# Decode attention over a streamed cache: the fourth K block in halves, finer waits at the first blocks, one more block in TensorE's loop, and Wo in five pieces

## The chip, the cores and the metric

One core of one Trainium2 chip. The metric is the device time of one execution in microseconds; a kernel's time is the median of its runs. The kernel before took 2521.9 us (median of three runs, 2521.62 to 2524.93).

## The reference, cut to what matters

One query token attends over a cache of 65,536 keys in each of 16 heads of size 256; a small gated MLP multiplies the result.

```python
xn = _layernorm(x)
q  = (xn @ wq).reshape(1, 1, 16, 256)              # x: 1 x 448
p  = softmax(einsum(q, k_cache) * 256 ** -0.5)     # k_cache, v_cache: 16 x 65536 x 256, bf16
s  = einsum(p, v_cache).reshape(1, 1, 4096) @ wo
g  = silu(silu(xn @ w1) @ w2)
out = x + s * g
```

The two caches are 1074 MB of the 1084 MB that come in. Every byte is used once.

## The kernel before

The caches are cut into 64 K blocks and 64 V blocks of 8.39 MB (128 partitions x 128 keys x 256 x bf16). Three buffers R[0..2] hold one block each. K block i goes into R[i % 3]; when its scores are done, **V block i is loaded over it**; when TensorE has summed V, K block i+3 is loaded over that. All loads are issued by SyncE on one queue, in the order K3 V2 K4 V3 K5 V4 ...

In the code `take` waits for a semaphore and takes off what it waited for; KB is 128 keys, HK 64 and SUB 32. The cuts leave lines out where `...` stands.

VectorE and ScalarE share the scores of a K block in four quarters of 32 keys: VectorE multiplies 13 keys in one wide product, which ScalarE then sums one by one, and does the other 19 (`ND`) itself. TensorE does the softmax's maximum, the query's broadcast and the 64 matmuls of a V block.

```python
def load_k(i, s):
    take(sp, vf[s])                      # TensorE has finished the V block in R[s]
    sp.dma_start(out=R[s][:, :], in_=block(Kd, i)).then_inc(kl[s], 16)
    sp.sem_inc(kh[s], 16)

def load_v(i, s):
    take(sp, kf[s])                      # VectorE has finished the K block in R[s]
    sp.dma_start(out=R[s][:, :], in_=block(Vd, i)).then_inc(vl[s], 16)

def dve_block(s, between=None):
    ...
    take(dve, kl[s], 16)
    for k in range(NSTEP):               # 4 quarters
        if k == NSTEP // 2:
            take(dve, kh[s], 16)
        ...                              # wide product for ScalarE, then ND products with sum
    # at the end: copy of S, .then_inc(kf[s], 1); maximum, .then_inc(rm, 1)

def pe_v(s):
    take(pe, pv)
    take(pe, vl[s], 16)
    pe_keys(psO, s, s, 0, KB, True, True, od)
    pe_mark().then_inc(vf[s], 1)
... # loads at the start, after w1 and wq
    load_keys(R[0], block(Kd, 0), 0, HK, kl[0])
    ...                                  # w2
    load_keys(R[0], block(Kd, 0), HK, KB, kh[0])
    load_k(1, 1)
    ...                                  # once w2 is used
    load_k(2, 2); load_v(0, 0); load_v(1, 1)
    # loop: load_k(i + s, s); load_v(i + s - 1, (s - 1) % NR)
... # the end: Wo in pieces of heads (0-5, 5-10, 10-14, 14-16) around the last parts of V63
    pe.wait_ge(wl[2], 16)
    project(h0, h0 + 2)                  # heads 10, 11
    t = pe_turn(tok=True)                # turns V63's sums
    ...
    project(h0 + 2, h1)                  # 12, 13
    pe.wait_ge(wl[3], 16)
    project(pieces[3][0], H1)            # 14, then 15 when its column is there
```

## Time and profile before

| | kernel before |
|---|---|
| time, median | 2521.9 us |
| span of the profiled run (its time was 2523.0) | 2521.1 us |
| bytes read | 1084.3 MB |
| share of the main DMA queue's packets in 16 engines' span | 99.6% |
| VectorE, ScalarE, TensorE busy | 89%, 57%, 46% |

The prediction below shows the lines and reads them: the DMA never rests but at the two ends and in two holes near 97 and 117 us. In the profile's lines PE is TensorE, PEld its weight loads, DVE VectorE, ACT ScalarE and SPq SyncE's queue. A window's line gives its length, then for PE, PEld, DVE, ACT and POOL (GpSimd) the busy time and the number of instructions, then TensorE's granted clock, the DMA's busy share and its GB/s.

One thing more is needed to follow the rest. A block's semaphore gets one increment from each of the sixteen DMA engines, and the trace records them singly: V0's sixteen came from 96.71 to 100.75 us in the kernel before. A packet of 65,536 bytes takes 2.42 us on its engine (the median of 15,872 in the trace of before), from the start to the end of the run, save the first ones after a pause (below). I call the time from the first to the last increment of a block the *spread*, and *the last engine* the one whose increment comes last. In these traces an engine that had fallen behind stayed behind: in the kernel before the spread was 1.5 us at every block from 199 to 335 us. It shrank where the others stood still, from 3.05 to 1.74 us from V1 to K3, at the hole. The consumer waits for the last engine (TensorE began with V0 at 100.64 us of the profile's time, 0.13 after its last increment), and the last landing of Wo stands in the chain that ends the run. Times of increments, here and in the prediction, count from a zero 0.24 us ahead of that of the profile's views; where the two are set against each other below, I have allowed for that; the prediction sets them against each other as they stand.

### The profile page before, as it was taken

The page shows a single profiled execution, that of the slowest core. Times are in us where ns is not written, and L with a number is a line of the kernel's source. Part 1 is how long each engine was busy: PE and PEld are TensorE (multiplying, and loading weights), DVE is VectorE, ACT ScalarE, POOL GpSimd, SP SyncE. Part 2 cuts the span into 40 slices and gives each one's busy share as a digit, 9 for nine tenths or more (in the row PEclk, how much of TensorE's full clock was granted, in tenths as well). Part 3 has the DMA queues.
Part 4 walks back from the last instruction along what each step waited for, and adds up shares of the span by engine and source line. Part 5 has one row for each costly group of instructions (what it writes and reads, how often), then busy time and mean ns, then how long its engine had stood idle before and what let it go on. Part 6 is the DMA issues. An engine that isn't in the chain of part 4 may idle for free. (4 is left out here: it accounts for less than half of the span.)

```text
span 2521.1 us, 29267 instructions
## 1 busy us (share of the span) xinstructions
PE 1151.9 (46%) x4738; PEld 438.2 (17%) x4738; DVE 2233.4 (89%) x10277; ACT 1445.9 (57%) x6996; POOL 1.9 (0%) x14
## 2 busy tenths in 40 slices
PE   3243544534535435345354353453543534534457
PEld 1111211111112112111121121121211211111122
DVE  6979889889898898898988988989989889889897
ACT  4656556556565565565655655655556556556564
POOL 0000000000000000000000000000000000000000
PEclk7666767767667677677676676766766767767678
DMA  9999999999999999999999999999999999999998
GB/s 424 402 433 433 433 433 433 434 432 433 435 434 436 435 436 434 434 433 434 435 433 433 433 433 433 433 433 433 433 436 435 436 436 434 434 433 435 433 423 353
DMA packets 22872, 1084.50 MB, mean 430 GB/s; under 512 B 2371, under 2 KB 4549, under 8 KB 4933
## 3 DMA queue, kind: packets, MB, share of 16 engines
q1 hardware_dynamic: 22850, 1084.30, 99.6%
q8 instruction: 5, 0.08, 0.0%
q14 instruction: 15, 0.11, 0.0%
q10 hardware_dynamic: 2, 0.00, 0.0%
HBM read 1084.29 MB, written 0.00 MB: 430 GB/s over the span
## 5 line engine op out<-in xcount | busy, mean ns | idle before, releaser
L276 ACT ACTIVATE R<-R 128x256 bf16<-128x256 bf16 x3328 | 1330.7, 401 | 754.4 <-ACTq L159 754.3
L254 DVE CUSTOM_DVE_ANT_0 R<-R,qcur 128x256 bf16<-128x256 bf16 x4864 | 1700.2, 417 | 0.0
L323 PE MATMUL bank<-R,PV 128*2 128x512 bf16 x4096 | 1032.1, 419 | 20.9 <-PEq L159 7.6
L243 DVE TENSOR_TENSOR R<-R,qcur 128x3328 bf16<-128x3328 bf16 x256 | 482.6, 1885 | 190.0 <-DVEq L159 189.9
L276 ACT ACTIVATION_READ_ACCUMULATOR R<-R 128x1 f32 x3328 | 619.9, 186 | 0.0
L335 PE MATMUL bank<-ident,rmax 128*1 128x128 bf16 x65 | 17.1, 263 | 1078.9 <-PEq L159 1078.9
L323 PEld LDWEIGHTS bank<-R,PV 128*2 128x2 bf16 x4096 | 367.3, 90 | 657.7 <-issue 218.4
L254 DVE DVE_READ_ACCUMULATOR2_ANT S<- 128x1 f32 x4864 | 384.1, 79 | 0.0
L335 PEld LDWEIGHTS bank<-ident,rmax 128*1 128x1 bf16 x65 | 5.2, 79 | 1083.4 <-issue 1083.3
L352 PE MATMUL bank<-eye,O 2*128 2x2 f32 x264 | 40.0, 252 | 231.3 <-PEq L159 231.3
L289 ACT ACTIVATE hist<-bank 128x1 f32 (+1 forms) x65 | 11.1, 171 | 204.4 <-ACTq L159 204.4
L352 PEld LDWEIGHTS bank<-eye,O 2*128 2x128 f32 x264 | 36.2, 207 | 248.6 <-issue 248.6
L219 DVE TENSOR_REDUCE gmax<-bank 1x1 bf16<-1x128 f32 x65 | 18.3, 281 | 38.1 <-DVEq L159 38.1
L236 DVE CAST qcur<-bank 128x256 bf16<-128x256 f32 x64 | 27.2, 425 | 24.6 <-DVEq L159 24.5
L310 ACT COPY hist<-bank 128x2 f32 (+1 forms) x66 | 10.5, 160 | 59.8 <-ACTq L159 59.8
L302 ACT COPY O<-bank 2x512 f32<-2x512 f32 x67 | 37.5, 559 | 12.4 <-ACTq L159 12.4
L291 ACT ACTIVATE PV<-S,hist 128x128 bf16<-128x128 f32 (+1 forms) x65 | 26.0, 399 | 13.4 <-ACTq L159 13.2
L366 PE MATMUL bank<-q,ident 8*128 (+1 forms) x63 | 24.3, 386 | 7.6 <-issue 1.7
L229 DVE COPY S<-S 128x128 f32<-128x128 f32 (+1 forms) x65 | 14.7, 226 | 9.5
L230 DVE TENSOR_REDUCE rmax<-S 128x1 bf16<-128x128 f32 (+1 forms) x65 | 18.2, 279 | 0.0
L341 PE MATMUL bank<-gmax,ones_row 1*128 1x1 bf16 x65 | 10.3, 158 | 4.6 <-PEq L159 0.9
L291 ACT ACTIVATION_READ_ACCUMULATOR PV<-S,hist (+1 forms) x65 | 12.1, 186 | 0.0
(68 smaller groups left out, 90.6 us busy)
## 6 DMA issues: line engine op xcount, KB each, us to landing
R<-in_A_k_cache_dram SPq DMA_DIRECT2D x4, 4096.0 KB, 24.2
R<-in_A_v_cache_dram SPq DMA_DIRECT2D x6, 2048.0 KB, 21.5
R<-in_A_wq_dram SPq DMA_DIRECT2D x1, 3072.0 KB, 12.7
R<-in_A_v_cache_dram SPq DMA_DIRECT2D x3, 1024.0 KB, 15.2
R<-in_A_wo_dram SPq DMA_DIRECT2D x2, 1120.0 KB, 18.4
R<-in_B_w_dram SPq DMA_DIRECT2D x1, 1568.0 KB, 27.1
R<-in_B_w_dram SPq DMA_DIRECT2D x1, 1344.0 KB, 5.8
R<-in_A_v_cache_dram SPq DMA_DIRECT2D x2, 512.0 KB, 16.4
```

The costliest lines, as they stand in the source:

```text
L219: dve.reduce_max(out=gmax[0:1, :], in_=ps_m[0:1, :], axis=AX.X).then_inc(gm, 1)
L230: dve.reduce_max(out=rmax[:, :], in_=S[:, c0:c1], axis=AX.X).then_inc(rm, 1)
L236: dve.tensor_copy(out=qcur[:, :], in_=ps_q).then_inc(sd, 1)
L243: m = dve.tensor_tensor(out=pair, in0=pair, in1=qcur[:, None, :].to_broadcast([P, NA, Dh]), op=ALU.mult,)
L254: ins = dve.tensor_tensor_reduce(out=Kv[:, c, :], in0=Kv[:, c, :], in1=qcur[:, :], scale=1.0, scalar=0.0, op0=ALU.mult, op1=ALU.add, accum ...
L276: ins = act.activation(out=prod, in_=prod, func=ACT.Identity, accum_out=S[:, c : c + 1],)
L291: act.activation(out=PV[s][:, c0:c1], in_=S2[:, c0:c1], func=ACT.Exp, bias=col(0, 1), scale=scale, accum_out=col(1, 2),).then_inc(pv, 1)
L302: act.copy(out=O[:, :], in_=po).then_inc(oc, 1)
L323: ins = pe.matmul(po, lhsT=PV[t][:, c : c + 2], rhs=R[s][:, c * Dh : (c + 2) * Dh], start=(start and c == k0), stop=(stop and c == k1 - 2),)
L335: pe.matmul(ps_m[0:1, :], lhsT=rmax[:, 0:1], rhs=ident[:, :], start=True, stop=True).then_inc(tm, 1)
L352: ins = pe.matmul(ps_t2[:, 2 * a : 2 * a + 2], lhsT=Ov[:, j, a, :], rhs=eye2[:, j, :], start=(j == 0), stop=(j == 1), is_transpose=True,)
L366: pe.matmul(ps_q, lhsT=ident[0:HP, at(j)].to_broadcast([HP, P]), rhs=q8[:, o : o + Dh] if isinstance(o, int) else q8[:, bass.ds(o, Dh)], s ...
```

## The change

Its intent: close the holes at the start by letting loads go out sooner, and leave less work behind the last landing.

```diff
-    def load_k(i, s):
+    def load_k(i, s, h=None):
+        if h is not None:
+            take(sp, h)                   # vh: half of V in R[s] is used
         take(sp, vf[s])
         sp.dma_start(out=R[s][:, :], in_=block(Kd, i)).then_inc(kl[s], 16)
+        sp.sem_inc(kq[s], 16)
         sp.sem_inc(kh[s], 16)
...
         for k in range(NSTEP):
+            if k == 1:
+                take(dve, kq[s], 16)
...
-    def pe_v(s):
+    def pe_v(s, k=KB, between=None):
         take(pe, pv)
         take(pe, vl[s], 16)
-        pe_keys(psO, s, s, 0, KB, True, True, od)
+        pe_keys(psO, s, s, 0, HK, True, False, vh[s])
+        pe_keys(psO, s, s, HK, k, False, k == KB, od if k == KB else None)
+        if between:
+            between()
+            pe_keys(psO, s, s, k, KB, False, True, od)
...
-        load_keys(R[0], block(Kd, 0), 0, HK, kl[0])
+        load_keys(R[0], block(Kd, 0), 0, SUB, kl[0])
+        load_keys(R[0], block(Kd, 0), SUB, HK, kq[0])
...
-        sp.sem_inc(vf[1], 1)
-        load_k(1, 1)
+        load_keys(R[1], block(Kd, 1), 0, HK, kl[1])
+        sp.sem_inc(kq[1], 16)
+        load_keys(R[1], block(Kd, 1), HK, KB, kh[1])
...
+        take(sp, vh[0])
+        load_keys(R[0], block(Kd, NR), 0, HK, kl[0])
+        sp.sem_inc(kq[0], 16)
+        take(sp, vf[0])
+        load_keys(R[0], block(Kd, NR), HK, KB, kh[0])
+        load_v(2, 2)                      # then the rest of the first pass, unrolled
...
-        with loop(pe, 1, LAST - 2, NR) as i: ...
-        pe_block(NBLK - 3, 0)
+        loop(pe, 1, NBLK - 3, NR, pe_block, more=1)   # a branch leaves in mid-body
         pe_turn()
-        pe_v(1)
-        pe_max(NBLK - 2)
+        pe_v(1, 96, lambda: pe_max(NBLK - 2))
...
-    pieces = cuts(0, 5, 10, 14, 16)
+    pieces = cuts(0, 5, 10, 12, 14, 16)
...
-        project(h0, h0 + 2)
+        project(h0, h0 + 1)               # head 10; then the turn; then 11
...
         pe.wait_ge(wl[3], 16)
-        project(pieces[3][0], H1)
+        project(*pieces[3])               # 12, 13
+        pe.wait_ge(wl[4], 16)
+        project(pieces[4][0], H1)         # 14
```

More of the change, by code (lines that the diff above doesn't have):

```diff
@@ L1 @@
-from contextlib import ExitStack, contextmanager
+from contextlib import ExitStack
 import concourse.bass as bass
@@ L162 @@
     kh = [sem(f"kh{t}") for t in range(NR)]
+    kq = [sem(f"kq{t}") for t in range(NR)]
     kf = [sem(f"kf{t}") for t in range(NR)]
@@ L165 @@
     vf = [sem(f"vf{t}") for t in range(NR)]
+    vh = [sem(f"vh{t}") for t in range(NR)]
     mr = sem("mr")
@@ L393, in pe_block, with loop @@
         pe_v(s)
-    @contextmanager
-    def loop(g, a, b, step):
+    def loop(g, a, b, step, block, more=0):
         es, name = {g.engine}, f"passes_{nc.next_id()}"
-        head, ann, body, tail = (f"{name}_{x}" for x in ("head", "ann", "body", "tail"))
-        assert (b - a) % step == 0
+        head, ann, body, rest, join, tail = (
+            f"{name}_{x}" for x in ("head", "ann", "body", "rest", "join", "tail")
+        )
+        assert (b - a) % step == 0 and more < step
+        last = b if more else b - step
         r = nc.alloc_registers(f"{name}_i", engines=es)
@@ L405, in loop, with go @@
         nc.br(head, engines=es)
+        def go(lo, hi):
+            i = nc.snap(r, min_val=a, max_val=last)
+            for s in range(lo, hi):
+                block(i + s, s)
         with nc.body(head, valid_engines=es):
-            g.br_eq(r, b - step, on_true=body, on_false=ann)
+            g.br_eq(r, last, on_true=body, on_false=ann)
         with nc.body(ann, valid_engines=es):
@@ L411, in loop @@
         with nc.body(body, valid_engines=es):
-            yield nc.snap(r, min_val=a, max_val=b - step)
+            go(0, more or step)
+            if more:
+                g.br_eq(r, last, on_true=join, on_false=rest)
+            else:
+                nc.br(join, engines=es)
+        if more:
+            with nc.body(rest, valid_engines=es):
+                go(more, step)
+                nc.br(join, engines=es)
+        with nc.body(join, valid_engines=es):
             nc.regs_alu(r, r, step, op=mybir.AluOpType.add)
-            g.br_lt(r, b, on_true=head, on_false=tail).branch_hint(hint)
+            g.br_lt(r, last + 1, on_true=head, on_false=tail).branch_hint(hint)
         nc.switch_bb(tail)
@@ L575 @@
         load_v(1, 1)
-        with nc.Fori(NR, LAST - 2, NR, engines={ET.SP}, head_slot={ET.SP: 0}) as i:
+        take(sp, vh[0])
[4 more added lines that the diff above has]
+        load_v(2, 2)
+        for s in range(1, NR):
+            load_k(NR + s, s, vh[s])
+            load_v(NR + s - 1, s - 1)
+        with nc.Fori(2 * NR, LAST - 2, NR, engines={ET.SP}, head_slot={ET.SP: 0}) as i:
             for s in range(NR):
-                load_k(i + s, s)
+                load_k(i + s, s, vh[s])
                 load_v(i + s - 1, (s - 1) % NR)
@@ L587 @@
         load_keys(R[0], Kl, 0, HK, kl[0])
+        sp.sem_inc(kq[0], 16)
         load_keys(R[0], Kl, HK, KB, kh[0])
@@ L601 @@
         load_wo(3)
-        with loop(dve, 0, LAST, NR) as i:
-            for s in range(NR):
-                dve_block(s)
-        with loop(act, 0, LAST, NR) as i:
-            for s in range(NR):
-                act_block(i + s, s)
+        load_wo(4)
+        loop(dve, 0, LAST, NR, lambda i, s: dve_block(s))
+        loop(act, 0, LAST, NR, act_block)
         def none(p):
@@ L623 @@
         pe_max(0)
-        with loop(pe, 1, LAST - 2, NR) as i:
-            for s in range(NR):
-                pe_block(i + s, s)
-        pe_block(NBLK - 3, 0)
+        loop(pe, 1, NBLK - 3, NR, pe_block, more=1)
         pe_turn()
-        pe_v(1)
-        pe_max(NBLK - 2)
+        pe_v(1, 96, lambda: pe_max(NBLK - 2))
         def weights(e0, e1, h0, h1, p_tot):
@@ L776 @@
         ))
-        project(h0 + 2, h1)
+        project(h0 + 1, h1)
         pe.wait_ge(wl[3], 16)
-        project(pieces[3][0], H1)
+        project(*pieces[3])
+        pe.wait_ge(wl[4], 16)
+        project(pieces[4][0], H1)
         need("pe", t_l)
```

## The prediction

> **What bounds the kernel now.** I read the page first, for the engine that never rests: the slices of the DMA and the row of its main queue.
>
> ```profile
> DMA  9999999999999999999999999999999999999998
> GB/s 424 402 433 433 433 433 433 434 432 433 435 434 436 435 436 434 434 433 434 435 433 433 433 433 433 433 433 433 433 436 435 436 436 434 434 433 435 433 423 353
> ...
> q1 hardware_dynamic: 22850, 1084.30, 99.6%
> ```
>
> The K and V caches (128 blocks of 8.39 MB) must come in once, and the sixteen DMA engines are busy for 99.6% of the span. The time is therefore bytes over rate plus whatever the DMA loses at the ends. Averaging 5 us windows from 200 to 2400 us gives 433.3 GB/s; 1084.3 MB at that rate take 2502.4 us. Of the 2521.1 us span only 18.7 us is not pure streaming, and that is all a change of order and waits can touch: 0.74%. Three slices are visibly low: the second (402) and the last two (423, 353).
>
> Next I cut the second slice into 5 us windows and read the last two columns, DMA share and GB/s.
>
> ```profile
> 90.00:95.00 5.00, 0.00 (x0) 0.00 (x0) 5.00 (x31) 4.18 (x22) 0.00 (x0) 0.50 0.97 419
> 95.00:100.00 5.00, 0.81 (x3) 0.28 (x3) 4.00 (x12) 1.18 (x6) 0.00 (x0) 0.50 0.83 301
> 100.00:105.00 5.00, 4.36 (x11) 1.37 (x12) 5.00 (x31) 4.78 (x24) 0.00 (x0) 0.50 1.13 487
> 105.00:110.00 5.00, 5.00 (x21) 1.72 (x19) 5.00 (x20) 2.14 (x11) 0.00 (x0) 0.85 1.04 447
> ...
> 115.00:120.00 5.00, 3.12 (x17) 1.45 (x15) 5.00 (x24) 1.43 (x6) 0.00 (x0) 1.00 0.73 262
> ```
>
> Two holes: 95 to 100 and 115 to 120 us. The timeline of SyncE's issues and of TensorE says what opened them.
>
> ```profile
> 60.32 35.82 SPq L202 DMA_DIRECT2D R<-in_A_v_cache_dram  x2
> 117.81 0.35 SPq L197 DMA_DIRECT2D R<-in_A_k_cache_dram  x1
> 131.68 0.34 SPq L202 DMA_DIRECT2D R<-in_A_v_cache_dram  x1
> ```
> ```profile
> 100.64 16.86 PE L323 MATMUL bank<-R,PV 128*2 128x512 bf16 x64 [3.59 <-PEq L159]
> ```
>
> V1, the second of the two merged V issues, goes out at 95.81 us, when VectorE has finished with K1. K3 goes out at 117.81, when TensorE has finished all 64 matmuls on V0, whose buffer K3 needs. Both issues come when the queue is nearly empty. The end I read in the chain of waits and TensorE's timeline.
>
> ```profile
> 2495.95 17.87 DMA R<-in_A_wo_dram
> 2513.82 0.04 issue
> 2513.87 0.92 PE bank L699 x4
> 2514.78 0.57 PE bank L352 x4
> 2515.35 1.62 PE bank L699 x8
> ```
>
> The end is a landing (a part of Wo) with sixteen small TensorE instructions, two VectorE operations and the output transfer behind it.
>
> [...] here the window at 100 shows PEclk 0.50 and 11 matmuls, that at 105 0.85 and 21. So the first half of V0 takes more than half of its 16.9 us.
>
> **The change part by part.** A lost microsecond counts only if the last of the sixteen engines loses it. So I compared the last increments of successive blocks: in steady state 19.35 us apart. At the start: K2 80.42, V0 100.75 (20.33), V1 120.35 (19.61), K3 141.08 (20.73), V2 160.44 (19.36). The medians of the sixteen tell another story: V1 lost 1.3 us and K3 2.7. The holes in the windows come to about 3 us of mean bandwidth, but for the last engine only 0.26 us at V1 and 1.38 at K3. V0's extra 0.98 us is of the one last engine alone (its median kept 19.34), so it is not starvation and the change does not touch it.
>
> First K in three parts, VectorE's wait by quarter. VectorE has its query at 22.08 + 0.42 = 22.5 us and then idles 3.76 us for half of K0 (first pass at 26.27). A quarter is 2.1 MB less, 4.8 us, so it should land at about 21.5, and VectorE starts at 22.5. The third quarter is needed 16.75 us later, at 39.3, but the second half's last increment is at 40.77, so about 1.4 us goes back. VectorE ends K0 and K1 some 2.3 us earlier; it then needs K1 at about 58, and K1 as a whole lands at 61.08, so K1 has to come in halves. V1 is then issued at about 93.5: **0.3 us** for the last engine.
>
> Fourth K in halves. V0 still lands at 100.75, so TensorE's start hardly moves. By the counts in the windows (11 by 105, 32 by 110) its first 32 matmuls end near 110. The first half of K3 goes out then, not at 117.81, 9 us ahead of V1's end; the second half at 117.5 has 4 MB in front of it. The hole at 115 closes: **1.4 us**.
>
> Steady state. One more wait of VectorE per block, one semaphore more on TensorE and SyncE. VectorE has 189.9 us of waits at its first pass (61 times, 3.1 each)[...]: 0.
>
> One more block in TensorE's loop: a branch taken where TensorE then waits for VectorE (1078.9 us over 64 blocks): 0. The maximum of block 62 moved into V61's matmuls: TensorE ended them at 2462.29 and served the maximum at 2462.32, while VectorE had been done since about 2460, so VectorE's last block can start about 2 us sooner. That shortens nothing alone, since the last V pieces land by the DMA, but keeps TensorE (busy from 2504.3 to 2513.6 without a pause to speak of) from being the bound once the DMA ends sooner.
>
> Wo in five pieces. The last two landed at 2514.07 and 2515.18; TensorE's last eight matmuls started at 2515.28 because the four matmuls of heads 10 and 11 and the turn ahead of them had waited for the four-head piece (2513.87 in the chain). With heads 10 and 11 landing about 1 us earlier, only heads 14 and 15, four matmuls (0.9 us), stay behind the last landing: 2515.2 + 0.9 = 2516.1 against 2516.96: **0.8 us**.
>
> Sum: 0.3 + 1.4 + 0.8 = 2.5 us[...]. 2521.9 - 2.4 = **2519.5 us**.
>
> **The rivals.** First, all bandwidth holes count: 3 us at the start, 0.9 at 2460 (357 GB/s in that window) and 1 to 2 at the end, giving 2516 to 2517. For it: the windows. Against: the last engine's increments. Second, nothing counts: the fast engines only run further ahead, the last one is as late as now, or TensorE's last V matmuls hold the end: 2521 to 2522. For it: V1's 0.26 is close to nothing, and one engine loses about 1 us at several places of the run for reasons outside the change. [...]
>
> **Range and chances.** My sum gives 2519.5; the first rival's best is 2516.5, the second's is 2522, and the three runs before spread over 3.3 us. I take 2517.3 to 2522.0. Two per cent is 50 us, which the 18.7 us outside streaming cannot yield[...]: faster 0.005, same 0.985, slower 0.01.
>
> **What would show it.** Right: first pass of VectorE near 22.5; V1 issued near 93.5; K3 as two issues near 110 and 117; over 400 GB/s in the windows at 95 and 115; K3's second half landing near 139.4; steady landings still 19.35 us apart; the last Wo landing near 2513.5 with four matmuls behind it[...]. Wrong: K3 landing near 141 in spite of an early issue (the last engine never starved), or a last landing that keeps its old time because later single-engine losses grew[...].

The three terms came to 2.5 us; an estimate of 0.1 us for one more transfer at the end made 2.4 of it, and so 2519.5. The 4.8 us for a quarter of K0 are an estimate, 2.1 MB at the measured 433.3 GB/s.

## The result, and the profile after

The changed kernel took 2521.79 us (median of four, 2521.33 to 2522.15) against 2521.98 of the kernel before in the same comparison (four, 2521.62 to 2524.93). The ratio is 0.9997, with a 95% interval of 0.9979 to 1.0014: the same. Ratios here are the mean time of one kernel's runs over that of the other's of the same rounds, so not quite the ratio of the medians quoted. Executions over 1.5% slower than the fastest of the same kernel are left out of the means. The span of the profiled run was 2519.6 us.

The page of the kernel after, the same rows and the two instruction queues:

```profile
DMA  9999999999999999999999999999999999999998
GB/s 423 422 440 423 427 432 432 427 433 433 433 435 435 433 434 434 435 434 436 435 434 433 433 433 433 433 433 433 433 433 433 433 433 433 434 435 434 434 428 359
...
q1 hardware_dynamic: 23298, 1084.30, 99.7%
q14 instruction: 14, 0.11, 0.0%
q8 instruction: 4, 0.07, 0.0%
```

The second slice rose from 402 to 422 GB/s. But the fourth, fifth and eighth (423, 427, 427), which had been at 433 and 434, fell. The instruction queues carry 18 packets; before it was 20.

The local steps came nearly as planned. Windows of the kernel after (last two columns: DMA share, GB/s); they had read 301 and 262, and over 400 was predicted for both, which the second misses:

```profile
95.00:100.00 5.00, 0.00 (x0) 0.00 (x0) 4.96 (x19) 3.42 (x17) 0.00 (x0) 0.50 1.04 419
...
115.00:120.00 5.00, 3.19 (x17) 1.47 (x15) 5.00 (x29) 1.36 (x5) 0.00 (x0) 1.00 0.90 387
```

SyncE's issues after (start, length of the merged pair): V0 and V1, then the two halves of K3, the first 7 us sooner than K3 had been:

```profile
58.08 35.82 SPq L207 DMA_DIRECT2D R<-in_A_v_cache_dram  x2
110.77 7.28 SPq L211 DMA_DIRECT2D R<-in_A_k_cache_dram  x2
```

VectorE's first three wide products after (the lines between them are left out): it begins at 22.00 instead of 26.27, and loses 1.94 us at the third quarter, where the second half has not landed:

```profile
22.00 1.89 DVE L250 TENSOR_TENSOR R<-R,qcur 128x3328 bf16<-128x3328 bf16 x1
30.38 1.89 DVE L250 TENSOR_TENSOR R<-R,qcur 128x3328 bf16<-128x3328 bf16 x1
40.77 1.89 DVE L250 TENSOR_TENSOR R<-R,qcur 128x3328 bf16<-128x3328 bf16 x1 [1.94 <-DVEq L159]
```

And the chain that ended last, after: no landing is in it any more, but the turn of V63's sums (their move from rows into columns, ready for Wo) and ten matmuls:

```profile
2512.84 0.61 PE bank L359 x4
2513.45 2.00 PE bank L734 x10
```

So where did the gain go? Last increments of landmarks in the two profiled runs, in us:

| last landing of | before | after | gained so far |
|---|---|---|---|
| K3 | 141.08 | 139.81 | 1.27 |
| the block 11 blocks on | 354.03 | 353.35 | 0.68 |
| the block 114 blocks after K3 | 2347.28 | 2346.65 | 0.63 |
| Wo | 2515.18 | 2514.50 | 0.68 |
| end of the span (profile's time) | 2521.1 | 2519.6 | 1.5 |

Half of the gain at K3 is given back between 140 and 354 us. The tail adds 0.8. That makes 1.5 us between these two runs, but the profiled run of before was about 1.1 us slower than its median and that of after 0.2 faster, so the medians show 0.2 us only. The third row depends on where it is cut: in the kernel before the very next block lands 1.12 us late (2367.75 against 2366.00, a gain of 1.75), behind an instruction packet of 16,384 bytes at 2353.6, which took 1.02 us, and between the 114th block and Wo both kernels take the same time (167.9 us).

In the kernel after, the spread at K3 is 4.0 us, before it was 1.7: the hole had made the faster engines wait for the last one. In the kernel after they keep their lead until V4, where the spread falls from 4.0 to 2.5 us. V4 is issued at 212.46, in the profile's time, 4.5 us ahead of the last landing before it:

```profile
212.46 0.33 SPq L207 DMA_DIRECT2D R<-in_A_v_cache_dram  x1
```

I put the packets of the trace together into sixteen chains, each packet behind the one that ended as it began. There eleven engines stand idle at V4's start, 0.1 to 1.4 us each; they begin 0.9 to 1.4 us after the issue, and their next packets take 2.8 to 3.5 us instead of 2.42. At later V starts single engines that had run out began anywhere from 1.0 to 3.6 us after the issue. An increment counts about 0.45 us after its engine's last data (here 0.44 to 0.50). So of the 4.5 us even the last engine has little to spare when the issue reaches it late, and one that leads has none.

### The profile page after: what moved, and what is told of

It reads as the page before. It is cut to its first block, busy times and chain, and to the rows that moved or that the text cites. A ratio compares the mean times of both kernels' runs of the same rounds, so it can differ in the third digit from the quotient of the medians.

```text
span 2519.6 us, 29489 instructions
## 1 busy us (share of the span) xinstructions
PE 1147.4 (46%) x4738; PEld 437.0 (17%) x4738; DVE 2233.5 (89%) x10277; ACT 1446.0 (57%) x6996; POOL 1.9 (0%) x14
## 3 DMA queue, kind: packets, MB, share of 16 engines
q1 hardware_dynamic: 23298, 1084.30, 99.7%
## 5 line engine op out<-in xcount | busy, mean ns | idle before, releaser
L250 DVE TENSOR_TENSOR R<-R,qcur 128x3328 bf16<-128x3328 bf16 x256 | 482.7, 1886 | 187.7 <-DVEq L159 187.5
```

Source lines behind the costliest of these rows:

```text
L250: m = dve.tensor_tensor(out=pair, in0=pair, in1=qcur[:, None, :].to_broadcast([P, NA, Dh]), op=ALU.mult,)
```

## The experiments

Two theories were to be told apart. **G**, given back: V goes out too late for engines that run ahead; once the hole at K3 is closed, the same waiting moves to the V blocks after it, and restarting engines overshoot, so that one of them becomes the new last. **S**, scatter: single engines lose about 1 us here and there for reasons outside the change, and that hides it. P in the expectations is the prediction. Their times per key are read in the trace of before: VectorE's own sums begin 0.345 us apart, and a wide product of 13 keys takes 1.885 us, about 0.145 a key; the first two quarters of K0 begin 8.4 us apart. Kernels of one call ran on the same chip with shared runs of the kernel before, whose medians were 2522.06 (e1 to e4), 2521.78 (e5 to e8), 2521.93 (e9 to e11) and 2522.06 (e12); the chip differed from call to call.

### e1: the changed kernel again

No edit.

> The changed kernel unaltered, a second trace and five more times beside the kernel before. Theory G (given back): K3's second half again lands last near 139.8 us against 141.1, the last engine's lead over the kernel before falls under 1 us by 350 us because the engines that ran ahead find no next V transfer, and the tail gains 0.8; in all 1.0 to 1.7 us, near 2520.6. Theory S (scatter): the two kernels' times overlap over five rounds, the difference is under 0.5 us, and the places where single engines lose about 1 us sit elsewhere in this trace than in the first one. Theory P (the prediction): 2.4 us less, 2519.5.

2521.80 us (five runs, 2521.1 to 2524.23), ratio 0.9999 (0.9985 to 1.0012). K3 landed at 139.91, as G says; but from K3 to the 114th block after it the last engine lost 3.9 us against 19.35 us per block, where the first trace had lost 0.9. (This trace is of the slowest of the five runs.) The losses all lie at the starts of V blocks or just after them, up to 550 us; engines that had run out there began 1.0 to 3.9 us after the issue. The expectation's 1.0 to 1.7 us of gain was a miss; S was right that the times overlap. The two theories meet here: the scatter is the giving back, and it differs from run to run. A window of this run at a V start:

```profile
290.00:295.00 5.00, 4.02 (x11) 1.29 (x12) 1.13 (x4) 0.67 (x3) 0.00 (x0) 0.50 0.95 367
```

### e2: only the fourth K in halves

```diff
-        load_keys(R[0], block(Kd, 0), 0, SUB, kl[0])          # and K1, pieces, pe_max as before
-        load_keys(R[0], block(Kd, 0), SUB, HK, kq[0])
+        load_keys(R[0], block(Kd, 0), 0, HK, kl[0])
+        sp.sem_inc(kq[0], 16)
```

> Only the fourth K in halves (with the new loops and quarter waits, whose semaphores it needs); first and second K, Wo in four pieces and block 62's maximum as before. Theory P: the last engine gains 1.4 us at K3 (lands near 139.7) and keeps it to the last Wo landing, the span falls by 1.4. Theory G: 1.0 to 1.4 gained at K3, at most 0.7 of it left at block 62. Theory S: 1.3 at K3, but the end differs by anything from -1 to +1.

2521.86 us (2521.28 to 2523.2), ratio 1.0000. K3 landed at 139.49, 1.6 us sooner than before, sooner even than in the whole change. So the parts at the first and second K add nothing for the last engine. Of the 1.6 us, 0.9 were left 114 blocks on (2346.40 against 2347.28), and 0.9 at the last Wo landing (2514.30).

### e3: only Wo in five pieces

```diff
-    pieces = cuts(0, 5, 10, 14, 16)
+    pieces = cuts(0, 5, 10, 12, 14, 16)     # with load_wo(4) and the new order of project
```

> Only Wo in five pieces, all else the kernel before. All landings of K and V as before to within 0.5 us unless single-engine losses differ. Theories P and G: from the last Wo landing to the end of the span 0.8 us less than the 5.9 us of before (2515.18 to 2521.1), time near 2521.2. A rival for the tail: the turn of V63's sums sets the end (it did in the changed kernel), so the part alone gives 0.3 or less.

From the last Wo landing (2516.90, which is 2516.66 in the profile's time) to the end of the span (2522.0) it took 5.3 us, for 6.1 before: the 0.8 us are real. In e2, which has four pieces, it was 6.2. The time was 2521.17 us (2520.91 to 2524.66): three runs near 2521.05 and two near 2524. The trace, of the run with 2523.92, shows the holes at V1 and K3 again (K3 at 141.43) and 1.6 us lost after K3. So the kernel before also loses time at V starts in some runs.

### e4: VectorE's share 18 of 32 keys

```diff
-ND = 19
+ND = 18
```

> The changed kernel with one key fewer of 32 summed by VectorE (18 for 19) and one more by ScalarE: VectorE's block shortens by about 4 x (0.345 - 0.14) = 0.8 us, so each V goes out about 5.2 us before the landing ahead of it, for 4.4. Theory G (the early V issues too late for engines that ran ahead): the lead of the first engine over the last settles near 2.4 us for 1.5, the losses of the last engine near 256 and 315 us vanish, K and V blocks land 0.7 us earlier from then on, and VectorE's last block ends 0.8 us sooner; time 2520 or less. Theory S: no change beyond 0.5 us.

2521.59 us (2521.08 to 2521.86), ratio 0.9998 (0.9984 to 1.0011). V goes out 5.3 us ahead instead of 4.5. The losses did not vanish (0.9 us from K3 on in the trace), so the expectation of 2520 was a miss, but no run was over 2522. The spread settled at 2.0 us for 1.2. Suggestive, not decisive.

### e5 and e6: V in halves, in the changed kernel and in the kernel before

```diff
     def load_v(i, s):
+        V = block(Vd, i)
+        take(sp, kg[s])        # VectorE and ScalarE are past the first three quarters of K
+        load_keys(R[s], V, 0, HK, vl[s])
         take(sp, kf[s])
-        sp.dma_start(out=R[s][:, :], in_=block(Vd, i)).then_inc(vl[s], 16)
+        load_keys(R[s], V, HK, KB, vg[s])   # TensorE waits for vg ahead of its second half
...                                          # VectorE's signal kg, and the same for V62
```

> The changed kernel, with each V block loaded in halves: the first half goes out when VectorE is in the last quarter of the K block whose buffer it takes (about 8 us sooner than now), the second half as now. Theory G (what the start gains is given back because V goes out only 4.4 us before the landing ahead of it): no engine idles at a V start from 213 to 650 us, the last engine's landings stay 19.35 us apart from K3 to block 60 in every trace, its lead of 1.3 over the kernel before stays whole; span near 2518.7, times 2520 to 2520.8 with less spread than the changed kernel's 2521.1 to 2524.2. Theory S (single-engine losses anywhere): times as the changed kernel's.

> The kernel before, with V in halves in the same way and nothing else. Theory G: the hole at K3 (1.4 us of the last engine) stays, since it comes of TensorE's late release; the small losses after it (up to 1.3 us in one trace of a kernel with the same loads) go; median 2521 to 2521.5, no run over 2522.5. Theory S: as the kernel before, 2521.5 to 2524.4. If it equals the changed kernel with V in halves, the early K3 is worth nothing even then.

e5 took 2525.72 us (2525.29 to 2526.09), e6 2526.14 us (2525.99 to 2526.26): slower by 4 us, and the expectations were wrong about the times. The trace says why. A packet of 32,768 bytes takes 1.215 us, so two take 2.430 for 2.420 of the large one; eight pairs in a V block make 0.07 us, and V blocks land 19.42 us apart instead of 19.35; 62 of them are 4.3 us. What theory G said of V's starts is seen all the same: V now goes out 11.2 us ahead, the last engine loses 0.1 us at V starts in e5 and 0.3 in e6, and the scatter fell from 3 us to 0.8 and 0.3. The 4 us also cover what I wanted to see of the start. And one more miss: in e6 K3 landed at 139.68 though it was loaded whole. TensorE could begin on V0's first half sooner (98.40 for 100.64 us), so K3 went out at 115.17 for 117.81.

### e7 and e8: V later by 1 and by 3 us

```diff
+            if not halves:
+                spent = Kv[:, SUB : SUB + 7, :]          # 21 in e8; these keys are no longer needed
+                dve.tensor_tensor(out=spent, in0=spent,
+                    in1=qcur[:, None, :].to_broadcast([P, 7, Dh]), op=ALU.mult)
             dve.tensor_copy(out=S2[:, c0:c1], in_=S[:, c0:c1]).then_inc(kf[s], 1)
```

> The changed kernel with one product of 7 keys more on VectorE (about 1.03 us, its result unused) ahead of the signal that frees each K buffer, so V goes out 3.4 us ahead instead of 4.4. By the trace a V issue takes about 1.2 us to its first packet[...]. Theory G: [...]the engines' spread is pressed below about 1 us early in the loop, the last engine loses more there (2 us or more in all), then nothing: 2522 to 2525. Theory S: unchanged.

> The same with 21 keys (about 3.0 us): V goes out 1.4 us ahead[...]. Theory G: [...]2585 to 2640, a window at V starts where all sixteen engines idle. A rival: [...]VectorE's 3.1 us of waiting per block takes it up, no more than 10 us slower.

e7 took 2552.75 us (2551.15 to 2554.37), ratio 1.0118 (1.0104 to 1.0133). e8 took 2576.45 us (median of five runs, 2561.69 to 2594.35), ratio 1.0207 (1.0181 to 1.0233); its sixth run, 2603.95, is left out. The extra products took 1.09 us in e7 and 2.96 in e8 (means in their traces). One microsecond later at each of some 60 V blocks cost 31 us in all, 0.5 us a block. Both times were misses: 2522 to 2525 was expected of e7, 2585 to 2640 of e8, and the rivals (unchanged; no more than 10 us) are refuted. I had expected the spread to be pressed together early and then nothing; in the trace of e7 the last engine loses 0.1 to 1.9 us at V starts all through the run. Both expectations rested on 1.2 us from issue to first packet and on a time from data to increment that was read wrongly (it is 0.45), e8's 2585 to 2640 with a loss per block reckoned from the two. And 1.2 is only the good case: in e7 and e8 engines that had run out began 1.0 to 5.1 us after the issue. Restarted engines come out unevenly, and the unevenness is what the next late V meets. With 3 us a window at such a start reads

```profile
1020.00:1025.00 5.00, 4.93 (x15) 1.63 (x16) 4.10 (x13) 2.48 (x12) 0.00 (x0) 0.62 0.71 288
```

The kernel, with VectorE waiting 3 us of every 38.7, thus stands within 1 us of a steep loss. V's issue is set by the end of VectorE's block, and that is the margin which the step "steady state: 0" of the prediction did not look at.

### e9 to e12: more room for V, without smaller packets

In all four VectorE sums fewer keys in the first three quarters and as many as before in the last, so that ScalarE doesn't end later than VectorE.

```diff
-ND = 19
+NDS = (15, 15, 15, 19)
...
+            ND, NA = NDS[k], SUB - NDS[k]     # in dve_block and act_sums
```

e9 is the changed kernel with these shares, e10 the kernel before with them, e11 is e2 (the fourth K in halves) with Wo in five pieces and the shares, e12 the kernel before with Wo in five pieces and the shares.

> The changed kernel, with VectorE summing 15 of 32 keys in the first three quarters of a block instead of 19 (ScalarE 17 for 13), the last quarter as it was. VectorE's block shortens by 3 x (4 x 0.345 - 4 x 0.145) = 2.4 us, so whole V blocks go out about 6.8 us ahead of the landing before them, for 4.4, at no cost in packets. Theory G: [...]no engine idles at a V start, the landings of the last engine stay 19.35 apart from K3 to block 60, its 1.3 us over the kernel before survive to the end, and with 0.8 at the tail the low runs are near 2520.0, median 2520.3, no run over 2521.5. Rival: the last engine's time is set by its own instruction fetches and packets whatever the V issues do; then 2521.1 to 2521.8, as with 18 of 32.

> The kernel before with the same shares. Here TensorE's release of V0's buffer sets K3, as before, so the hole at K3 stays (VectorE faster by 2.4 us a block brings V1 out earlier, but V0 lands when it lands): K3's last landing 140.5 to 141.1. Theory G: the scatter goes (no run over 2522.3), median 2521.3 to 2521.8; against the changed kernel with these shares it is then 1.3 to 2.1 slower, which is the change's worth when it is not given back. Rival: both the same within 0.5.

> Of the change only the fourth K in halves, the new loops and Wo in five pieces, with the same shares; the first K in two parts, the second whole, block 62's maximum after V61 as before. If the parts at the first and second K and the moved maximum are worth nothing, as the traces so far say, this equals the changed kernel with the shares within 0.4 us. If they matter once VectorE is quick, it is 0.5 to 1 slower.

> The kernel before with the shares and Wo in five pieces: all of the eleventh run but the fourth K in halves (and the new loops). Theory G as amended: with VectorE quicker the late K3 costs the last engine nothing (it landed at 139.70 in the tenth run, 139.68 in the eleventh), and Wo in five pieces takes 0.8 off, so the low runs are near 2519.9. If the fourth K in halves is what keeps away the runs 2 us above the others (two of five in the tenth run, none in the ninth and eleventh), one or two such runs come here again; if not, all five lie within 0.7 of one another and the fourth K in halves is worth 0.5 us or less.

| kernel | K3 in halves | Wo in five | times of five runs | median | ratio, 95% interval |
|---|---|---|---|---|---|
| e9 | yes | yes | 2519.51 to 2520.19 | 2519.76 | 0.9988, 0.9974 to 1.0001 |
| e10 | no | no | 2520.62, 2520.65, 2520.76, 2522.45, 2522.6 | 2520.76 | 0.9995, 0.9981 to 1.0008 |
| e11 | yes | yes | 2519.15 to 2519.78 | 2519.36 | 0.9986, 0.9972 to 1.0 |
| e12 | no | yes | 2519.59, 2519.86, 2521.74, 2521.75, 2522.54 | 2521.74 | 0.9994, 0.998 to 1.0008 |

V goes out 7.0 us ahead in all four. e9 and e11 met their expectations (e9's median came 0.5 us lower, and a few single engines idled at V starts). e10 missed its numbers: K3 landed at 139.70 for 140.5 to 141.1, the median was lower than 2521.3, and two runs were over 2522.3. e12's low runs came as expected, its late K3 did not. In e9 V4 is issued at

```profile
210.09 0.33 SPq L206 DMA_DIRECT2D R<-in_A_v_cache_dram  x1
```

and the window in which e1 had 367 GB/s reads, in e9,

```profile
290.00:295.00 5.00, 5.00 (x21) 1.78 (x20) 0.29 (x1) 0.00 (x0) 0.00 (x0) 0.83 1.02 433
```

The last engine's loss from K3 to the 114th block after it (time between the two landings less 114 x 19.35), in one trace of each kernel:

| kernel | V ahead, us | K3 landed | lost after K3 | last Wo landing |
|---|---|---|---|---|
| before | 4.5 | 141.08 | 0.3 | 2515.18 |
| after | 4.5 | 139.81 | 0.9 | 2514.50 |
| e1 (after again) | 4.5 | 139.91 | 3.9 | 2517.19 |
| e9 (after, shares) | 7.0 | 139.99 | 0.0 | 2512.78 |
| e11 (K3 and Wo, shares) | 7.0 | 139.68 | 0.1 | 2512.47 |
| e10 (before, shares) | 7.0 | 139.70 | 0.4 | 2512.97 |
| e12 (Wo, shares) | 7.0 | 141.53 | 0.5 | 2514.85 |

With room for V the lead of the engines does no harm: the spread stays near 3.6 us to the end in e9 and nothing is lost up to the 114th block. So far theory G holds. The shares do more than it said, though. From the 114th block to Wo the six traces with V 4.5 or 5.3 us ahead (before, after, e1 to e4) took 167.4 to 168.0 us, the four with 7.0 took 166.8 to 166.9. So about 1.0 us of what the shares give arises there, also in e10, which is 1.2 us faster than the kernel before without the fourth K in halves. In the kernel before 1.12 us of that stretch is the late block behind an instruction packet; at the same packet e10 and e12 lose nothing. Why the shares spare it isn't shown.

The experiment yields a kernel that is faster than both, though by 0.1% only: e11, whose five runs all lie below every run of the kernel before (2521.21 at the least), by 2.6 us in the median. Its interval just reaches 1.0; nine runs of the kernel before went from 2521.65 to 2526.92.

The pair e11 and e12, though on two chips (medians of the kernel before 2521.93 and 2522.06), shows what the fourth K in halves is worth. Without it the hole at 117 us is there in both traces (236 GB/s in e10's window), and e12's reads

```profile
115.00:120.00 5.00, 3.08 (x17) 1.41 (x15) 5.00 (x20) 1.46 (x6) 0.00 (x0) 1.00 0.65 223
```

but in e10 the last engine was still at work when K3 came and lost nothing, and in e12 it stood idle too and lost 2.0 us. So the hole costs 0 to 2 us by the run. What differs is when TensorE is done with V0, for K3 goes out then. Its 64 matmuls took 15.29 us in e10 (granted clock 0.64 from 100 to 105 us, then 1.00), 15.93 in e3, 16.70 in e12 (0.50, then 0.87) and 16.86 in the kernel before (0.50, then 0.85). K3 went out at 116.48, 117.04, 117.77 and 117.81, and the last engine lost 0.0, 1.1, 2.0 and 1.4 us. These are four traces; no experiment varied it. The runs split likewise, three low and two high in e10, two low and three high in e12; where the fourth K is in halves and V has room (e9, e11), no run is high. That the high runs are those in which the hole hurts was seen in one trace of each kind only (e10's was a low run, e12's one of the high ones).

e9 is 0.4 us slower than e11, which lacks the parts at the first and second K and the moved maximum, and their ranges overlap. Those parts are not worth anything here.

## Why the prediction was right or wrong

The range and the class were right; the middle was 2.3 us too low, and the sum of small gains did not arrive: 0.2 us of 2.4. That the range held is no credit to the mechanism: the result lies 0.2 us below its upper end, and a change worth nothing (2521.9) would have lain in it too. Of the signs named in advance, those at the start came true, but the window at 115 us had 387 GB/s and not over 400, the last Wo landing came at 2514.50 and not near 2513.5, and ten matmuls and not four stood at the end.

- **What bounds.** Right. The queue's share stayed at 99.6 to 99.7%, and blocks landed 19.35 us apart.
- **First and second K, 0.3 us.** The mechanics came to within 0.5 us: VectorE began at 22.0 (22.5 predicted), lost 1.9 us at the third quarter (1.4), and V1 went out at 93.6 (93.5). The worth did not: V1 landed at 120.39, for 120.35 before, and e2 without these parts has K3 no later.
- **Fourth K in halves, 1.4 us.** Right at K3: the halves went out at 110.8 and 117.7, and K3 landed 1.27 us earlier (1.6 in e2). The comparison with one trace hid that the hole costs 0 to 2 us by the run.
- **"Steady state ... 0".** This is the step that failed. I had looked at VectorE's waits (3.1 us a block; with the change they are 187.5 us in all for 189.9) and not at what ends with VectorE's block: the issue of V. It left 4.5 us to the last landing before it, of which the issue needs 1.0 to 3.9 and the increment 0.45; engines more than 3 us ahead (the spread was 4.0) had to stand still even in the best case. The hole had been the place where they did so; when it was closed they did so at V4 and after, and those that restarted late became the last. Measured up to the 114th block: 0.9 and, in a run 2.4 us slower than its kernel's median, 3.9 us of the last engine, against 0.3 before, and 0.0 to 0.1 with V 7 us ahead and K3 in halves (e9, e11). Before is one trace here, and in e3, whose loads are those of before, 1.6 us were lost too, so the difference between the kernels is less sure than the effect of V's room.
- **TensorE's loop and the maximum of block 62: 0 by themselves.** Right. VectorE's last block did begin about 2 us sooner in its place in the run: at 2460.1, 2.4 after the end of block 62.
- **Wo in five pieces, 0.8 us.** The size was right: 5.3 us for 6.1 behind the last landing; 5.4 in e9 and 6.1 in e10 with the shares. There was luck in it. The sum set 2515.2, an increment's time, against 2516.96 of the profile's; with one zero it gives 1.1. And the path was another: not four matmuls behind the last landing but TensorE's turn of V63's sums and ten matmuls, which end 1.2 us behind that landing, for the predicted 0.9.
- **The rivals.** The second, "nothing counts", came nearest in time, and one of its reasons, losses of single engines, was half the truth: those at V starts were not outside the change, those behind instruction packets are in the kernel before as well (1.12 us at one packet). The first, that all holes count, is refuted by K3, whose median increment came 3.4 us sooner and the last 1.3.
- **The base.** The 1.4 us were read in a run 1.1 us slower than its kernel's median, and taken off the median. A loss that is seen in one such run should not be taken off a typical one.

Left open: how often TensorE is late enough with V0 for the hole at K3 to cost something in the kernel before, of which there is one trace, and so how the 0.2 us between the medians is made up; and why the shares save about 1.0 us behind the 114th block.

## What to carry to other kernels

Where the DMA is the bound, as here with its queue at 99.6%, follow the last of the sixteen engines, not the mean bandwidth (K3's median increment came 3.4 us sooner, its last 1.3), and ask of every load how long before the queue runs dry it is issued: here the hole that was closed let the fast engines run ahead (a spread of 4.0 us for 1.7) to the next load that was issued late. Before closing a hole at the start, give the load of the steady state more room; here a few sums moved from VectorE, which released the buffer, to ScalarE, which was 57% busy, took 2.0 us off the changed kernel (e9) and 1.2 off the kernel before (e10), and smaller loads that gave still more room cost 4 us. A change of half a per mille (1.3 us here) needs several traces on both sides, since one engine's luck moved the time by as much: the fourth K's hole cost the last engine 0.0 to 2.0 us in four traces.
